# Grouping the row sums with the similarities at the head of an attention pair, and moving the weight sums of the first expert turn

## The chip, the cores and the metric

The kernel runs on one core of a Trainium2 chip. The metric is the device time of one execution in microseconds (us); lower is better. Engines are named as the profile names them: PE is TensorE's matmuls, PEld its weight loads, DVE is VectorE, ACT is ScalarE, POOL is GpSimd, SP is SyncE, which issues most DMAs. [...]

## The reference

Two blocks follow each other. The first is attention with clusters, over 4 batches, 8 heads, 768 positions and 64 features. Each query and each key is assigned to the nearest of 16 centroids, and a query sees only keys of its own cluster. The second is a mixture of experts: each of the 3,072 rows goes to one of 8 experts, which are two matmuls with a ReLU between, and the result is scaled with the gate's weight.

```python
q_assign = np.argmax(np.einsum('bhsd,hcd->bhsc', q_n, c_n), axis=-1)
k_assign = np.argmax(np.einsum('bhsd,hcd->bhsc', k_n, c_n), axis=-1)
mask = q_assign[:, :, :, None] == k_assign[:, :, None, :]
scores = scale * np.matmul(q, k.transpose(0, 1, 3, 2))
scores = np.where(mask, scores, -1000000000.0)
...
attn = attn / (np.sum(attn, axis=-1, keepdims=True) + 1e-09)
return np.matmul(attn, v).astype(np.float32)
...
logits = x @ w_gate
expert_idx = np.argmax(logits, axis=1)
...
for e in range(E):
    h = np.maximum(x_sorted[lo:hi] @ w1[e], 0.0)
    y_sorted[lo:hi] = h @ w2[e]
```

Here x is the attention's output, with the 8 heads of a row side by side (512 features).

## The kernel before

**Pairs.** Attention works on 16 pairs of heads: 4 batches times 4 pairs (`NPAIR`, `HP` = 4). Pair n holds two heads on the two halves of the partitions. Its queries are taken in two halves h (384 columns), its keys in six blocks j (128 each), so a pair has 12 units (h, j), numbered u = 0 to 11. One unit of `score` is four f32 matmuls of queries and keys and two bf16 matmuls that add the mask (all L433), and then an exp on ACT (L445) into a tile A. `add_up` (L451, DVE) adds A into ACC, for the sums over the keys; it runs for all j but 0. After the 12 units come 12 of `attend` (L457), six for each half, each half ended by a copy of the result O from PSUM to the tile oT on ACT (L464).

**What is done beside the pair.** A table, `AT`, holds further steps under (pair, place), and the loop over pairs runs them through `between(n, u)` after unit u; place 12 lies between the two halves of the attends, 13 behind them. The steps are:

- `prepare(n, step)`, for the pair that comes next. Step 0 turns the loaded q and k on DVE (L277, `turn`); step 1 is the matmuls with the centroids (L291, `similar`); step 2 transposes their result out of PSUM and compares it with its maximum (`assign0`, `assign1`, L302 to L311, DVE); step 3 makes the cluster codes ohT (`assign2`, L318 to L327, DVE); steps 4 and 5 copy the codes into the mask tiles mk (L340) and mq (L337), four ACT instructions each. The score's mask matmuls read mk and mq. Step 0 of pair n + 2 is issued in the loop itself, at place 12 of pair n.
- the end of an earlier pair. `sum_up` (L480, 24 PE instructions) forms the softmax sums from ACC and the gate's logits from oT; `weights_of` (L489 to L504, DVE) reads them; `rows` (L510, DVE) turns oT, and `store` (L517, SP) writes it to HBM.
- the gate of a finished batch b: `gate`, `gate_exp` (ACT), `gate_sum`, `choose` (DVE), then `count` (L592, L593, two small matmuls) and `number` (L598 to L607), which gives each row its place in the list of its expert and scatters the row's number to HBM from POOL.
- the preparation of the first expert turn (below).

**PSUM.** The pool `ps_s` has three double banks for scores, so the scores are at most three units ahead of the exps. The pool `ps_m` has two banks for similarities, sums and O. A new tile takes the bank that is released first in the program's order, and waits for that bank's readers. `count` writes into the bank of the latest sums (`BANK`).

**Expert turns.** After attention, 10 turns work through the experts. Turns 0 and 1 take up to 288 rows each of the two fullest experts, from the first three batches. A turn needs: the experts' ranking (`rank_first`, DVE), the list of its rows and the two weights (`first_turns`: `expert`, `places`, `fetch1`, `fetch2`, all on SP), the row indices (`indices`, L728, L729), the gather (`gather`, L738, POOL), the rows times their softmax and gate weights (`weigh`, L755), a way through HBM that splits them (`take`, L771), `turn_rows` (L780, DVE) and the sums and differences that save a matmul in eight (`x_sums` and `w1_sums`, L789, DVE; w1_sums makes A[0] to A[3], where A[1] needs A[2] and A[3] needs A[1]). All of this is placed in pairs 13 to 15 for turn 0.

`layer1` of a turn is 2 x 7 products (L968), with a hook after each, to which steps are tied by number. In turn 0 these hold the sums of pair 15, the gate of batch 3, its count and its numbering. In the first half the products use, in this order: w1 itself, A[2], A[1], w1, A[0], w1, A[3]. The last one adds into a bank that DVE reads first (L926 at L1007).

The loop of the pairs:

```python
for n in range(NPAIR):
    if n + 2 < NPAIR:
        load(n + 2)
    for h in range(2):
        for j in range(NQ):
            score(n, h, j)
            if j:
                add_up(n, h, j)
            between(n, h * NQ + j)
    for h in range(2):
        for j in range(NQ):
            attend(n, h, j)
        if h == 0:
            between(n, 12)
            prepare(n + 2, 0)
    between(n, 13)
```

Of the kernel before, what the change touches and what calls it, by code (L numbers as in the profile page):

```python
# [33 lines left out]
def kernel(  # L34
# [11 lines left out]
    nc = tc.nc  # L46
    B, H, S, D = q.shape
# [8 lines left out]
    HP = H // 2  # L56
    NPAIR = B * HP
# [28 lines left out]
    wa = ctx.enter_context(tc.tile_pool(name="weights_a", bufs=1))  # L86
    w1s = ctx.enter_context(tc.tile_pool(name="w1_sums", bufs=1))
    xp = ctx.enter_context(tc.tile_pool(name="rows", bufs=1))
    accp = ctx.enter_context(tc.tile_pool(name="accp", bufs=3))
    otp = ctx.enter_context(tc.tile_pool(name="otp", bufs=2))  # L90
    stat = ctx.enter_context(tc.tile_pool(name="stat", bufs=2))
    rt = ctx.enter_context(tc.tile_pool(name="route", bufs=1))
# [75 lines left out]
    with tc.manual_schedule(), ExitStack() as actx:  # L168
# [655 lines left out]
        def at_pair(n, u, f, *a):  # L824
            AT.setdefault((n, u), []).append(lambda: f(*a))

        for n in range(NPAIR):
            if n:
                at_pair(n, 2, sum_up, n - 1)
                at_pair(n, 4, rows, n - 1)  # L830
                at_pair(n, 4, store, n - 1)
            for u, step in ((2 if n else 6, 1), (5 if n else 7, 2), (7 if n else 8, 3), (11, 4), (11, 5)):
                at_pair(n, u, prepare, n + 1, step)
        for b in range(B - 1):
            n = HP * (b + 1)
            last = b == B - 2
            at_pair(n, 5 if last else 10, gate, b)
            at_pair(n, 8 if last else 11, gate_exp, b)
            at_pair(n + (not last), 9 if last else 3, gate_sum, b)
            at_pair(n + (not last), 10 if last else 9, choose, b)  # L840
            at_pair(n + 2 - last, 2, count, b)
            at_pair(n + 2 - last, 3 if last else 6, number, b)
        for n in range(1, NPAIR):
            at_pair(n, 2, weights_of, n - 1)
        n = HP * (B - 1)
        slots = range(len(EARLY))
        at_pair(n + 1, 4, rank_first)

        def first_turns():
            for s in slots:  # L850
# [3 lines left out]
            GR[0]["w1"] = fetch1(GR[0]["e"], wa)  # L854
            GR[0]["w2"] = fetch2(GR[0]["e"], wa)

        at_pair(n + 1, 6, first_turns)
        for s in slots:
            at_pair(n + 1, 13, indices, s)
        at_pair(n + 2, 6, gather, 0)  # L860
        at_pair(n + 2, 13, weigh, 0)
        at_pair(n + 3, 1, take, 0)
        at_pair(n + 3, 4, turn_rows, 0)
        at_pair(n + 3, 6, x_sums, 0)
        at_pair(n + 3, 9, w1_sums, 0, (2, 1), nc.vector)
        at_pair(n + 3, 13, w1_sums, 0, (0, 3), nc.vector)

        def between(n, u):
            for f in AT.pop((n, u), ()):
                f()  # L870
# [4 lines left out]
        for n in range(NPAIR):  # L875
            if n + 2 < NPAIR:
                load(n + 2)
            for h in range(2):
                for j in range(NQ):
                    score(n, h, j)  # L880
# [5 lines that stand above are left out]
                    attend(n, h, j)  # L886
                if h == 0:
                    between(n, 12)
                    prepare(n + 2, 0)
            between(n, 13)  # L890
        assert not AT

# [1 line left out]
    with tc.manual_schedule(), ExitStack() as ectx:  # L894
# [262 lines left out]
        n = NPAIR  # L1157
        last = NS - 1
# [6 lines left out]
        def second_weights(s):  # L1165
            GR[s]["w2"] = fetch2(GR[s]["e"], (wa, wb)[s % 2])

        for s in range(NS):
            h1, h2 = {}, {}

            def at(d, i, f, *a):
                d.setdefault(i, []).append(lambda: f(*a))

            if s == 0:
                at(h1, 2, sum_up, n - 1)
                at(h1, 2, weights_of, n - 1)
                at(h1, 3, gate, B - 1)
                at(h1, 3, gate_exp, B - 1)
                at(h1, 5, gate_sum, B - 1)
                at(h1, 5, choose, B - 1)  # L1180
                at(h1, 8, count, B - 1)
                at(h1, 9, number, B - 1)
                at(h1, 11, rows, n - 1)
                at(h1, 11, store, n - 1)
                at(h1, 12, rank_all)
                at(h2, 0, rank_rest)
                at(h2, 3, places, 2)
                at(h2, 3, first_weights, 2)
                at(h2, 5, places, 3)
                at(h2, 7, indices, 2)  # L1190
                at(h2, 7, gather, 2)
            if s == 3:
                at(h1, 12, ask)
                at(h2, 4, answer)
            if s < last:
                if s == 0:
                    first_weights(1)
                elif s > 1:
                    take(s + 1)
                if s == 1:  # L1200
                    at(h1, 6, weigh, 2)
                    at(h1, 7, take, 2)
                    at(h1, 8, second_weights, 2)
                else:
                    second_weights(s + 1)
                if 0 < s <= last - 2:
                    at(h2, 0, first_weights, s + 2)

                if 0 < s <= last - 3:
                    at(h2, 1, places, s + 3)  # L1210

                if s == 0:
                    when = ((h2, 1), (h2, 2), (h2, 5), (h2, 6), (h2, 7), (h2, 7))
                elif s == 1:
                    when = ((h1, 9), (h1, 12), (h2, 2), (h2, 3), (h2, 6), (h2, 6))
                else:
                    when = ((h1, 9), (h1, 10), (h2, 1), (h2, 2), (h2, 2), (h2, 5))
                if GR[s + 1]["T"] >= 2 * P:
                    for (h, i), f, a in zip(when, (w1_sums,) * 4 + (w2_sums,) * 2, (2, 1, 0, 3, 2, 0)):
                        at(h, i, f, s + 1, (a,), nc.vector)  # L1220
                at(h2, 1 if s == 1 else 3, turn_rows, s + 1)
                if GR[s + 1]["T"] >= 2 * P:
                    at(h2, 1 if s == 1 else 4, x_sums, s + 1)
            if s == 0:
                at(h1, 2, gather, 1)
                at(h1, 8, weigh, 1, slice(0, 1))
                at(h1, 11, weigh, 1, slice(1, 2))
                at(h1, 12, weigh, 1, slice(2, 3))
                at(h1, 12, take, 1)
            elif s + 2 <= last:  # L1230
                at(h1, 5 if s == 2 else 4, indices, s + 2)
                at(h1, 5 if s == 2 else 4, gather, s + 2)
                at(h2, 6 if s == 1 else 4, weigh, s + 2)
            if pairs_of(s):
                at(h1, 4, w2_sums, s, (1,), nc.vector)

                at(h1, 5 if s == 1 else 6, w2_sums, s, (3,), nc.vector)
            if s == last - 1:

                at(h1, 4, nc.gpsimd.drain)  # L1240
            (layer1 if GR[s]["T"] >= 2 * P else few_columns)(s, h1)
            h_sums(s)
            layer2(s, h2)
# [271 lines left out]
```

## Time and profile before

| what | us |
|---|---|
| time, median of 3 runs | 660.87 |
| the runs, lowest and highest | 659.3, 662.08 |
| the profiled execution, its own time | 659.27 |
| the profiled execution, its span | 657.5 |
| PE busy | 644.2 (98% of the span) |
| DVE busy | 490.0 (75%) |
| ACT busy | 338.8 (52%) |
| POOL busy | 130.8 (20%) |
| start of pair 1; of turn 0's first layer | 31.8; 329.5 |

The span is the time from the first to the last instruction of the profiled execution; the execution's own time also holds what lies around it. A busy engine isn't one at its peak: the ends of matmuls are modelled, so lengths of PE work are best taken from one start to the next start. TensorE's granted clock was full throughout (0.998). Attention is the first half of the span, the expert turns are the second half.

### The profile page before, as it was taken

Reading aid. Unit: us, or ns where it says so; the run is one execution under the profiler, and the core shown is the slowest. Engines: PE = TensorE matmul, PEld = TensorE weight load, DVE = VectorE, ACT = ScalarE, POOL = GpSimd, SP = SyncE. Lnnn points to the kernel's source line nnn. Section 1 sums busy time; section 2 is a strip of 40 time slices with the busy share of each in tenths; the row PEclk is TensorE's granted clock in tenths of the full one; section 3 lists DMA queues with packets and bytes.
Section 4 is the critical chain, followed back from the end, with each engine's and each line's share of the span. In section 5 each row is a group of like instructions: output and inputs, shape, how many; then the busy total and the mean of one; then the engine's idle time right before and its main releaser. Section 6 shows DMA issues by size and latency. Waiting matters only on the chain.

```text
span 657.5 us, 11491 instructions
## 1 busy us (share of the span) xinstructions
PE 644.2 (98%) x4252; PEld 423.3 (64%) x4252; DVE 490.0 (75%) x845; ACT 338.8 (52%) x584; POOL 130.8 (20%) x166
## 2 busy tenths in 40 slices
PE   8999999999999999999999999999999999999996
PEld 4444544455444454544484979989797987869773
DVE  6988888998889988989887997888869365572300
ACT  4677878768878777867532333333231331323210
POOL 4500000022000300041103522324240422140010
PEclk9999999999999999999999999999999999999999
DMA  7663455443355433347475587776684835614010
GB/s 150 150 120 68 76 94 97 72 80 68 73 97 98 74 76 72 72 132 227 117 273 156 187 314 264 252 275 211 249 307 170 273 138 165 233 74 173 7 49 19
DMA packets 189760, 95.38 MB, mean 145 GB/s; under 512 B 152895, under 2 KB 171839, under 8 KB 188416
## 3 DMA queue, kind: packets, MB, share of 16 engines
q1 hardware_dynamic: 184624, 81.56, 45.2%
q0 software_dynamic: 4928, 12.97, 6.1%
q8 instruction: 35, 0.57, 0.4%
q14 instruction: 29, 0.24, 0.1%
q10 hardware_dynamic: 144, 0.03, 0.0%
HBM read 74.10 MB, written 20.70 MB: 144 GB/s over the span
## 4 chain that ended last, share of the span: by engine, by line
PE 80%; issue 10%; DVE 5%; POOL 2%; ACT 1%; DMA 1%; POOLq 0%; DVEq 0%; ACTq 0%
PE sps L433 20%; PE mps L457 16%; PE bank L968 10%; PE sbank L968 8%; PE bank L1069 7%; PE bank L1088 7%; PE sbank L1069 6%; PE mps L480 2%; PE mps L291 1%; PE bank L937 1%; DMA xg<-x_rows,gi 1%; DVE xT L780 1%; POOL tokens_of L607 1%; DVE acc L451 1%; DVE a L789 1%
## 5 line engine op out<-in xcount | busy, mean ns | idle before, releaser
L445 ACT ACTIVATE A<-sps 128x768 f32<-128x768 f32 x192 | 152.1, 814 | 30.0 <-PE sps L433 29.4
L433 PE MATMUL sps<-qT,kT 64*128 64x384 f32 x768 | 158.9, 492 | 0.0
L451 DVE TENSOR_TENSOR acc<-acc,A 128x768 f32<-128x768 f32 x128 | 121.4, 948 | 11.4 <-ACT A L445 2.9
L457 PE MATMUL mps<-A,v_in 128*64 128x384 f32 x768 | 127.4, 488 | 0.0
L433 PEld LDWEIGHTS sps<-qT,kT 64*128 64x128 f32 x768 | 66.8, 187 | 52.2 <-issue 48.4
L457 PEld LDWEIGHTS mps<-A,v_in 128*64 128x64 f32 x768 | 53.7, 137 | 70.6 <-issue 62.9
L1043 POOL DMA_INDIRECT out_dram<-z,si x30 | 47.7, 1590 | 196.0 <-DVE z L926 167.2
L607 POOL DMA_INDIRECT tokens_of<-tg,pos_i x24 | 27.5, 1147 | 270.5 <-DVE pos_i L605 264.4
L433 PE MATMUL sps<-mq,mk 64*128 64x384 bf16 x384 | 64.9, 323 | 3.1 <-ACT mq L337 1.3
L1088 PE MATMUL bank<-w,h 128*128 128x512 f32 (+2 forms) x224 | 64.4, 596 | 0.0
L340 ACT ACTIVATE mk<-ohT,kscn,ksc 32x384 bf16<-32x384 bf16 x60 | 42.0, 700 | 40.5 <-DVE ohT L327 39.7
L968 PE MATMUL bank<-xT,w 128*128 128x144 f32 (+4 forms) x288 | 47.7, 309 | 0.0
L738 POOL DMA_INDIRECT xg<-x_rows,gi x30 | 38.4, 1280 | 47.0 <-DVE si L729 16.4
L968 PE MATMUL sbank<-xc,a 128*128 128x144 f32 (+4 forms) x288 | 47.7, 309 | 0.0
L1088 PEld LDWEIGHTS bank<-w,h 128*128 128x128 f32 (+2 forms) x224 | 24.6, 151 | 32.5 <-issue 32.3
L968 PEld LDWEIGHTS bank<-xT,w 128*128 128x128 f32 x288 | 43.8, 190 | 2.6 <-issue 2.2
L451 DVE TENSOR_TENSOR acc<-A 128x768 f32<-128x768 f32 x32 | 30.4, 952 | 19.2 <-ACT A L445 19.1
L968 PEld LDWEIGHTS sbank<-xc,a 128*128 128x128 f32 x288 | 43.4, 190 | 0.0
L926 DVE TENSOR_TENSOR h<-sbank,p 128x288 f32<-128x288 f32 (+4 forms) x18 | 9.2, 514 | 45.7 <-PE sbank L968 45.5
L433 PEld LDWEIGHTS <-mk 64*128 64x128 bf16 x384 | 19.9, 94 | 29.0 <-DVE mk L383 2.6
L986 ACT ACTIVATE h<-h 128x288 f32<-128x288 f32 (+4 forms) x36 | 17.6, 488 | 38.1 <-DVE h L926 38.1
L755 DVE TENSOR_TENSOR xw<-xg,sf 128x256 f32<-128x256 f32 (+2 forms) x60 | 32.8, 606 | 0.9 <-DMA xg<-x_rows,gi 0.6
(216 smaller groups left out, 900.5 us busy)
## 6 DMA issues: line engine op xcount, KB each, us to landing
w<-in_moe_w_dram SPq DMA_DIRECT2D x20, 2048.0 KB, 10.7
v_in<-in_v_dram SPq DMA_DIRECT2D x32, 192.0 KB, 2.5
x_rows<-x SPq DMA_DIRECT2D x64, 96.0 KB, 2.4
turn_rows<-xw SPq DMA_DIRECT2D x23, 256.0 KB, 2.0
q_in<-in_q_dram SPq DMA_DIRECT2D x60, 96.0 KB, 3.2
k_in<-in_k_dram SPq DMA_DIRECT2D x60, 96.0 KB, 3.2
xs<-turn_rows SPq DMA_DIRECT2D x16, 144.0 KB, 2.8
xs<-turn_rows SPq DMA_DIRECT2D x8, 208.0 KB, 4.2
```

The costliest lines, as they stand in the source:

```text
L340: nc.scalar.activation(dst, src, AF.Identity, bias=less, scale=big)
L433: nc.tensor.matmul(SP[n, h, j][:, a, 0:HS], lhsT=kt[rows, j * P : (j + 1) * P], rhs=qt[rows, h * HS : (h + 1) * HS], start=first, stop=not ...
L445: nc.scalar.activation(A[n, h, j], ps[:, :, 0:HS], AF.Exp, scale=D**-0.5)
L451: nc.vector.tensor_tensor(ACC[n, h], first, A[n, h, j], op=ALU.add)
L457: nc.tensor.matmul(O[n, h][D * a : D * (a + 1), 0:HS], lhsT=VIN[n][:, a, j, :], rhs=A[n, h, j][:, a, :], start=(j == 0), stop=(j == NQ - 1),)
L607: ins = nc.gpsimd.indirect_dma_start(out=t_d[:, :], out_offset=bass.IndirectOffsetOnAxis(ap=pos_i[:, i : i + 1], axis=0), in_=tg[:, b, i, ...
L738: nc.gpsimd.indirect_dma_start(out=xg[0:m], out_offset=None, in_=x_d[0:rows_in, :], in_offset=bass.IndirectOffsetOnAxis(ap=g["gi"][0:m, j ...
L755: nc.vector.tensor_tensor(xw[0:m, :, :, d2 * a : d2 * (a + 1)], xg[0:m].rearrange("p (r a d b) -> p a r b d", r=HP, a=2, b=DB)[:, a], g["s ...
L968: nc.tensor.matmul(ps[:, f * T2 : (f + 1) * T2], lhsT=w[:, k, (2 * j + f) * P : (2 * j + f + 1) * P], rhs=x[:, k, :], start=first and f + ...
L1043: ins = nc.gpsimd.indirect_dma_start(out=out[:, :], out_offset=bass.IndirectOffsetOnAxis(ap=GR[s]["si"][0:rows, j : j + 1], axis=0), in_=z ...
L1069: nc.tensor.matmul(ps[:, 0:H], lhsT=x[:, k, :], rhs=y[:, k, :], start=first and k == 0, stop=k == 3, skip_group_check=not first,)
L1088: nc.tensor.matmul(ps[i * m : (i + 1) * m, :], lhsT=h[:, f, j * P : j * P + m], rhs=w[:, f, :], start=(k == 0), stop=(k == FB // n - 1),)
```

## The change

Seven things change, all of them places of work; no instruction's work itself is changed.

1. There is a new place, -1, ahead of a pair's first score (`between(n, -1)`).
2. In pairs 2 to 11 `sum_up` of the pair two back and `similar` of the next pair are issued at place -1. `weights_of` follows at 0, `rows` and `store` at 3. The steps assign0/1, assign2 and the turn of pair n + 2 are at 2, 4 and 9 (before: 5, 7, 12). For this, ACC has four buffers instead of three. In pair 1 nothing is summed.
3. Pair 12 sums pair 10 at -1 (its rows at 0), and then pair 11 at 2, with the similarities. From pair 13 on a pair sums the one before it at 2, as before the change; `weights_of` comes at 3 there.
4. The gates of batches 0 and 1 come about one pair later, with `count` at place 2 of pairs 7 and 11.
5. `rank_first` and `first_turns` in pair 13 move from 4 and 6 to 9 and 11, `indices` from the end of pair 13 to place 2 of pair 14; `weigh` and `take` are issued at 11 and 13 of pair 14.
6. In pair 15 the weight sums A[2], A[1], A[0], A[3] are at 1, 2, 3, 4 (before: two at 9, two at 13), `turn_rows` and `x_sums` at 6 and 7 (before: 4 and 6).
7. In turn 0 the sums of pair 15 and their weights move from hook 2 to hook 3, the gate of batch 3 from hook 3 to hook 4.

```diff
-    accp = ctx.enter_context(tc.tile_pool(name="accp", bufs=3))
+    accp = ctx.enter_context(tc.tile_pool(name="accp", bufs=4))
...
+        LATE = HP * (B - 1)
+
+        def pair_end(n, u, v, m):
+            at_pair(n, u, sum_up, m)
+            at_pair(n, u + 1, weights_of, m)
+            at_pair(n, v, rows, m)
+            at_pair(n, v, store, m)
+
         for n in range(NPAIR):
-            if n:
-                at_pair(n, 2, sum_up, n - 1)
-                at_pair(n, 4, rows, n - 1)
-                at_pair(n, 4, store, n - 1)
-            for u, step in ((2 if n else 6, 1), (5 if n else 7, 2), (7 if n else 8, 3), (11, 4), (11, 5)):
-                at_pair(n, u, prepare, n + 1, step)
+            if n >= 2 and n <= LATE:
+                pair_end(n, -1, 3 if n < LATE else 0, n - 2)
+            if n >= LATE:
+                pair_end(n, 2, 5 if n == LATE else 4, n - 1)
+            if n == 0:
+                steps = (6, 7, 8, 11, 11, 12)
+            elif n == 1 or n >= LATE:
+                steps = (2, 5, 7, 11, 11, 12)
+            else:
+                steps = (-1, 2, 4, 11, 11, 9)
+            for step, u in enumerate(steps):
+                at_pair(n, u, prepare, n + 1 + (step == 5), (step + 1) % 6)
         for b in range(B - 1):
             n = HP * (b + 1)
             last = b == B - 2
-            at_pair(n, 5 if last else 10, gate, b)
-            at_pair(n, 8 if last else 11, gate_exp, b)
-            at_pair(n + (not last), 9 if last else 3, gate_sum, b)
-            at_pair(n + (not last), 10 if last else 9, choose, b)
-            at_pair(n + 2 - last, 2, count, b)
-            at_pair(n + 2 - last, 3 if last else 6, number, b)
-        for n in range(1, NPAIR):
-            at_pair(n, 2, weights_of, n - 1)
+            if last:
+                when = ((n, 5), (n, 8), (n, 9), (n, 10), (n + 1, 2), (n + 1, 3))
+            else:
+                when = ((n + 1, 10), (n + 1, 13), (n + 2, 3), (n + 2, 9), (n + 3, 2), (n + 3, 6))
+            for (m, u), f in zip(when, (gate, gate_exp, gate_sum, choose, count, number)):
+                at_pair(m, u, f, b)
         n = HP * (B - 1)
         slots = range(len(EARLY))
-        at_pair(n + 1, 4, rank_first)
+        at_pair(n + 1, 9, rank_first)
...
-        at_pair(n + 1, 6, first_turns)
+        at_pair(n + 1, 11, first_turns)
         for s in slots:
-            at_pair(n + 1, 13, indices, s)
+            at_pair(n + 2, 2, indices, s)
         at_pair(n + 2, 6, gather, 0)
-        at_pair(n + 2, 13, weigh, 0)
-        at_pair(n + 3, 1, take, 0)
-        at_pair(n + 3, 4, turn_rows, 0)
-        at_pair(n + 3, 6, x_sums, 0)
-        at_pair(n + 3, 9, w1_sums, 0, (2, 1), nc.vector)
-        at_pair(n + 3, 13, w1_sums, 0, (0, 3), nc.vector)
+        at_pair(n + 2, 11, weigh, 0)
+        at_pair(n + 2, 13, take, 0)
+
+        for u, i in enumerate((2, 1, 0, 3)):
+            at_pair(n + 3, u + 1, w1_sums, 0, (i,), nc.vector)
+        at_pair(n + 3, 6, turn_rows, 0)
+        at_pair(n + 3, 7, x_sums, 0)
...
                 load(n + 2)
+            between(n, -1)
             for h in range(2):
...
                     between(n, 12)
-                    prepare(n + 2, 0)
             between(n, 13)
...
             if s == 0:
-                at(h1, 2, sum_up, n - 1)
-                at(h1, 2, weights_of, n - 1)
-                at(h1, 3, gate, B - 1)
-                at(h1, 3, gate_exp, B - 1)
+                at(h1, 3, sum_up, n - 1)
+                at(h1, 3, weights_of, n - 1)
+                at(h1, 4, gate, B - 1)
+                at(h1, 4, gate_exp, B - 1)
```

## The prediction

> **What bounds the kernel now.** I read the page's busy shares first: PE 98%, DVE 75%, ACT 52%. So the end is set by TensorE's stream, and only two things can move it: work that PE does, and places where PE stands. The chain of waits, narrowed to one ordinary pair, shows the stream (start, length, in us):
>
> ```profile
> 170.20 2.62 PE sps L433 x18
> 172.82 1.11 PE mps L480 x24
> 173.93 0.65 PE mps L291 x8
> 174.58 7.47 PE sps L433 x54
> 182.05 7.89 PE mps L457 x48
> 189.94 0.84 PE sps L433 x3
> ```
>
> One pair is 3 score units, sums (L480), similarities (L291), 9 score units, 12 attends: 19.74 us, nothing else on the chain. Next, busy time in five stretches: pair 8, pair 13, pair 14, pair 15, and the first layer of turn 0.
>
> ```profile
> core 0: us, PE busy (x) PEld busy (x) DVE busy (x) ACT busy (x) POOL busy (x), PEclk, DMA share, GB/s
> 170.13:189.87 19.74, 19.74 (x155) 9.66 (x153) 17.05 (x29) 15.59 (x23) 0.00 (x0) 1.00 0.46 83
> 268.96:288.84 19.88, 19.88 (x156) 9.77 (x154) 18.21 (x45) 11.90 (x18) 6.77 (x6) 1.00 0.21 45
> 288.84:310.37 21.53, 20.21 (x154) 9.89 (x152) 19.49 (x37) 17.47 (x27) 4.58 (x4) 1.00 0.76 254
> 310.37:329.47 19.10, 19.10 (x146) 9.41 (x145) 15.88 (x27) 11.70 (x17) 2.26 (x2) 1.00 0.40 100
> 329.47:347.20 17.73, 16.76 (x144) 15.13 (x143) 14.69 (x37) 6.08 (x16) 2.04 (x3) 1.00 0.68 253
> ```
>
> Only pair 14 (21.53) and turn 0 lose time; every other pair is full, and DVE is at 17 to 19 of 19.7, so it has little room. The timelines of ACT, DVE and PE say why (idle time before the row in brackets):
>
> ```profile
> 287.43 2.85 ACT L340 ACTIVATE mk<-ohT,kscn,ksc 32x384 bf16<-32x384 bf16 x4 [5.56 <-DVE ohT L327]
> ```
> ```profile
> 290.86 0.32 PE L433 MATMUL sps<-mq,mk 64*128 64x384 bf16 x1 [1.10 <-ACT mq L337]
> ```
> ```profile
> 338.75 1.25 PE L968 MATMUL sbank<-xT,a 128*128 128x144 f32 x8 [0.71 <-DVE h L926]
> ...
> 342.16 0.17 PE L592 MATMUL mps<-last,lt_b 128*128 128x8 bf16 x1 [0.21 <-DVE last L586]
> ```
>
> In pair 13 DVE gives the cluster codes (ohT) late, ACT copies them into the mask late, and pair 14's first mask matmul stands. Its three scores take 4.42 (288.84 to 293.26) for the usual 2.62: 1.8 us lost. In turn 0, PE waits behind DVE's queue.
>
> [...]score units start 0.807 us apart (155.68, 156.49, 157.29), so nine are 7.26, but the stretch of nine takes 7.47 and that of three 2.62 instead of 2.42. Each separate run of scores costs 0.20 to 0.21. [...]ACT stood 5.56 us before a mask copy with other work behind it. [...]
>
> **Part 1, the head group, pairs 2 to 11.** Sums (of pair n-2) and similarities stand before the first score, so attend, sums, similarities and twelve scores follow. Scores: 12 x 0.807 + 0.21 = 9.89 instead of 2.62 + 7.47 = 10.09. The 128-row group keeps its 1.76, attends their 7.89 (the same 7.89 stands before L902, another mode, so its exit doesn't depend on the follower). Pair: 19.54. Gain 0.20 x 10 = 2.0 us. Bounds from the bubble: 0.1 to 0.3 each.
>
> Does the head stand on something? Sums take the bank of O(h=0), freed by ACT's copy after the eight mask copies (5.0 us). With the assigns at 2 and 4, DVE reaches the codes after four adds instead of six: first add at 4.6 after the head, once two exps exist (weights_of, 1.35, lies before it), then four adds of 0.87, or 1.05 where the next one depends on it, assigns 1.67 and 2.07, rows 0.89: 12.9. Copies run 13.0 to 18.0, O(0) is out at 18.4, the next head is at 19.5: no wait. Similarities need O(1)'s copy, 0.65 after the head (329.58 + 0.48 against 329.47), and come at 1.0: no wait. Their turn, at u = 9, comes after four more adds and ends at 18.5. No cover is left if codes slip by 1.1 us.
>
> **Part 2, count of batches 0 and 1** moves to pairs 7 and 11 at u = 2, now alone inside scores. Today it costs 0.14 beside the similarities (134.89 to 135.03) in pairs 6 and 10. Alone it also splits scores: 0.14 + 0.20. Net +0.40 (between +0.2 and +0.8).
>
> **Part 3, sums moved over pairs.** Pair 1 loses its sums: 1.76 becomes 0.78 (pair 0's similarities alone), -0.98. Pair 12 gets an extra head of sums alone, 1.11 as in pair 15. Net +0.13.
>
> **Part 4, pairs 12 to 14.** Pair 12 does two pairs' ends. weights_of(10) and rows(10), 2.24 us of DVE, fit into its idle 1.68 before the first add plus its wait for the fourth exp. But weights_of(11) now follows add 3 instead of filling that wait. From add 3 DVE never idles: today 255.62 to 272.11, the second turn's end, is 16.49. With weights_of 1.35 more, 17.84, starting at 1.11 + 2.62 + 1.76 + 2.01 = 7.50 after the head, it ends at 25.34; pair 13 starts at 1.11 + 19.74 = 20.85. Hence: mask copies start 3.01 before pair 13 (codes at 7.50 + 10.23, plus 0.11). Today a start 1.41 before pair 14 costs 1.79, so the break is 3.20: stall 0.19. Sums follow 2.81 into the pair, similarities at 3.81, but the turn ends at 4.49: stall 0.74. Together +0.93.
>
> Pair 13: score 4 starts 5.46 in, add 3 at 7.47. Then add 0.87, weights_of 1.08, number 1.35, add 0.88, rows 0.90, add 0.87, assign 1.74, add 0.87, assign2 2.06: codes at 18.09 (rank_first, 2.18, now behind them). The pair lasts 19.74 + 0.14 + 0.93 = 20.81; copies start 2.66 before its end: stall 0.54. Adds 1.90, rank 2.18, adds 1.90: sums wait until 3.32 into pair 14 (0.16), similarities until turn(15)'s end at 5.06 + 0.06 (0.80). Together 1.50, against 1.79 today: -0.29.
>
> Moved DMAs. first_turns follows the ranking (at 22.2 of pair 13). Its register loads, four list loads and two weight loads took 287.49 to 291.35 until the second list landed; with about 1.5 for register reads no longer hidden by the token wait, that is 6.9 into pair 14. SP's x_rows store of pair 13 comes at 12, so nothing stands behind. Indices reach DVE at 6.9: no margin, but DVE then waits for exp 4 at 7.9, which hides 0.3. Gather landed 9.75 after its index (293.49 to 303.24), so 17.5, weigh at 21.5. w1 took 7.4: 12.5 into pair 14, wanted 4.5 into pair 15. Take and weigh keep their place on DVE; SP's take still precedes store(14).
>
> **Part 5, pair 15 and turn 0.** Four weight sums of 1.22 go between adds, turn_rows waits no more for its DMA (2.48 of DVE today). DVE ends its last add 23.5 after the pair's start; sums at hook 3 start at 23.7. Today: 333.16 to 334.82 = 1.66 for 1.11, so 0.55 goes. Then c (338.75): before it 0.88 is lost; weights_of now lies beside the product and gate behind the add, 0.1 remains. But DVE's weights_of-to-choose chain took 6.25 (335.86 to 342.11), still about 6.0, and PE now reaches the count 5.0 after it: about 1.05 for 0.21 today. Net -0.55 - 0.78 + 0.84 = -0.5 (from -1.3 to 0). Experts after that keep their order: nothing.
>
> **Sum.** -2.0 + 0.40 + 0.13 + 0.93 - 0.29 - 0.5 = -1.3 us. The profiled execution took 659.27 (span 657.5 plus 1.8 around it), so 657.9; it is the low end of the runs, whose median is 660.87, so the median goes to 659.5.
>
> **Rivals.** (B) The late pairs come out clean: the 0.93 of pair 13, the 1.50 of pair 14 and 0.2 of the count wait don't appear, because the spread of rank and sums lets DVE get by. For it: each is a wait of under 1 us, so a DVE order 1 us quicker removes nearly all. Against: 17.8 us of DVE work without a gap. -1.3 - 2.6 = -3.9: 657.0.
> (C) Slower: DVE stands before indices in pair 14 for a late list. Price: lists on a loaded queue take 10.0 us to land by the page instead of 1.8 to 2. That is 8 later; DVE absorbs 1, and codes for pair 15 have 0.65 to spare (copies start 3.85 before it, break 3.20), so PE loses about 6.4: 660.87 - 1.3 + 6.4 = 666.0. It ends slower than before once the lists are 3 us late, by over 0.5% once 6.3. Against it: the loads are issued ahead of the weights.
> (D) The change doesn't do what it says: [...]part 1 is nothing: +0.7, 661.6. Against it: 7.89 before L902.
>
> **Numbers.** Forecast 0.42, B 0.38, C 0.10, D 0.10. B gets this much since DVE tallies of three loaded pairs multiply small errors, and all of them are waits that a little shift removes. Half a percent is 3.3 us, about what a measurement of this kernel tells from no change. Forecast and D fall within: 0.52; B faster: 0.38; C slower: 0.10. The forecast's own range is 658.0 to 661.0. The range 655.8 to 662.0 takes in B, D and both ends of parts 1, 2 and 5, and leaves C out.
>
> **What would show it.** Part 1: pairs 2 to 11 at 19.54, one score stretch of 9.9, no PE gap before L480. Part 2: 19.9 in pairs 7 and 11. Part 4: waits of L291 for the turn (L277) at pairs 13 and 14, and mask waits under 1. Part 5: L480 in turn 0 at 1.1, a longer wait at L592. Wrong, if a head pair stays at 19.7, if PE waits for ACT's copy (L464) in the heads, or if the lists land late.

## The result, and the profile after

The changed kernel took 662.29 us (median of 13 runs, 661.33 to 663.20) beside 660.87 of the kernel before (13 runs, 658.64 to 662.08): ratio 1.0028, 95% interval 1.0018 to 1.0038, or by the medians 1.4 us longer where 1.3 less was forecast. That is one comparison. A second one of the same two kernels gave 658.48 for 659.45: ratio 0.9987 (interval 0.9980 to 0.9995; ratios below are to the kernel before in the same comparison and are written in this way). A third gave 663.06 for 660.47: 1.0034 (1.0025 to 1.0043). The second and the third ran on two different chips; on which the first ran is not known. Most of what follows is about why they differ.

The page of the profiled execution of the first comparison (span 660.6, own time 662.30), its busy shares and its chain that ended last:

```profile
PE 645.3 (98%) x4252; PEld 424.2 (64%) x4252; DVE 488.7 (74%) x845; ACT 340.2 (51%) x584; POOL 131.9 (20%) x166
PE 76%; DVE 15%; ACT 4%; issue 2%; DMA 1%; SPq 1%; DVEq 0%; POOL 0%; POOLq 0%; ACTq 0%
```

TensorE is as busy as before. DVE's share of the chain is 15%; in the second comparison's profile of the same kernel it is 9%. Where the time goes is seen in busy time of the stretches that the prediction showed (pairs 8, 13, 14, 15, first layer of turn 0; the columns are those of the table shown there):

```profile
168.50:189.63 21.13, 19.82 (x155) 9.68 (x153) 17.12 (x26) 14.99 (x22) 3.08 (x4) 1.00 0.42 76
269.44:290.74 21.30, 21.09 (x156) 10.05 (x155) 18.94 (x41) 15.02 (x23) 7.15 (x6) 1.00 0.33 62
290.74:312.11 21.37, 21.16 (x155) 10.11 (x153) 18.31 (x43) 14.39 (x22) 4.48 (x4) 1.00 0.66 236
312.11:332.44 20.33, 19.57 (x147) 9.62 (x145) 19.89 (x30) 13.36 (x21) 2.26 (x2) 1.00 0.51 116
332.44:349.06 16.62, 16.02 (x143) 14.99 (x142) 12.01 (x36) 5.99 (x16) 2.04 (x3) 1.00 0.71 270
```

The same stretches of the same kernel in the second comparison (span 656.4):

```profile
168.12:187.66 19.54, 19.54 (x155) 9.72 (x153) 17.12 (x27) 15.39 (x22) 3.07 (x4) 1.00 0.46 83
267.46:288.30 20.84, 20.84 (x157) 9.97 (x155) 18.47 (x40) 14.59 (x22) 7.14 (x6) 1.00 0.30 58
288.30:309.67 21.37, 21.16 (x155) 10.12 (x153) 18.86 (x44) 15.02 (x23) 3.94 (x4) 1.00 0.65 235
309.67:329.45 19.78, 19.57 (x146) 9.61 (x145) 19.39 (x30) 13.05 (x20) 2.31 (x2) 1.00 0.53 121
329.45:346.08 16.63, 16.03 (x144) 15.00 (x143) 12.03 (x36) 6.00 (x16) 2.05 (x3) 1.00 0.71 270
```

Turn 0 and pair 14 agree to 0.01 us. Pair 8 differs by 1.59, pair 13 by 0.46, pair 15 by 0.55. With 0.35 in pair 2 and 1.15 in turn 3 (both below) this is all of the 4.1 us between the two spans. The chain of waits around pair 8's head (start, length, what), first comparison:

```profile
168.57 1.11 PE mps L480 x24
169.69 0.65 PE mps L291 x8
170.33 3.07 PE sps L433 x18
173.40 0.01 issue
173.41 0.82 ACT A L445
174.22 0.04 issue
174.27 7.54 PE sps L433 x54
```

and second comparison:

```profile
168.19 1.11 PE mps L480 x24
169.30 0.65 PE mps L291 x8
169.95 9.89 PE sps L433 x72
```

In the second the head is what Part 1 predicted: one stretch of twelve score units, 9.89. In the first, the fourth score unit waits for the first exp (L445), which began at 173.41 although the last matmul of its scores had started at 171.02; in the second it began 0.4 us behind that matmul. TensorE was on time, ScalarE heard of it 2 us late. VectorE did too: the transposed sums (L489) came 2.46 us after the last matmul of the sums, 0.71 in the second.

One more thing sets the two profiles apart, in the landing times of DMAs. First comparison and second:

```profile
w<-in_moe_w_dram SPq DMA_DIRECT2D x20, 2048.0 KB
```
```profile
w<-in_moe_w_dram SPq DMA_DIRECT2D x20, 2048.0 KB, 11.9
```

The first has no landing times, because records of semaphore updates are missing in it. (Such a record in the profile gives the time at which an engine or a DMA reported that something is ready.) 7,984 updates are recorded, for 8,909 in the second and 8,966 in the kernel before's profile. Most of the missing ones are DMAs' (5,909 for 6,770), but PE, ACT and DVE lack 13, 14 and 32 too. Of these three engines' 1,722 updating instructions 49 have no record within 0.4 us of their end. All 49 lie within 0.5 us of an indirect transfer of POOL (token scatters L607, gathers, row writes), where only 405 of the 1,722 lie. All nine profiles here from three chips (those of the third comparison, of scatter_over_9 and of turns_9) lost hundreds of records in this way; in each of the eight from two others at most two engine updates lack theirs.

The records that are there also show where the 2 us come from: TensorE's updates themselves are late. At this head its last sums, its similarities and its first three score units ended at 169.69, 170.33, 171.34, 172.15 and 172.95; its updates are recorded at 171.80, 173.25, 173.32, 173.40 and 173.47, and the exp began 0.09 us after the third of these, its own. In the second profile every one is recorded within 0.04 us of the end. VectorE's and ScalarE's recorded updates at the first profile's head are on time (within 0.03 us). The same holds throughout: up to 650 us, updates recorded more than 0.15 us behind the end of the last instruction that can have made them are TensorE's alone, 3 to 20 of them in each of the ten profiles with losses, and none in the nine without.

### The profile page after: what moved, and what is told of

The parts are those of the page before. It is cut to its first block, busy times and chain, and to the rows that moved or that the text cites. A ratio compares the mean times of both kernels' runs of the same rounds, so it can differ in the third digit from the quotient of the medians.

```text
span 660.6 us, 11502 instructions
## 1 busy us (share of the span) xinstructions
PE 645.3 (98%) x4252; PEld 424.2 (64%) x4252; DVE 488.7 (74%) x845; ACT 340.2 (51%) x584; POOL 131.9 (20%) x166
## 4 chain that ended last, share of the span: by engine, by line
PE 76%; DVE 15%; ACT 4%; issue 2%; DMA 1%; SPq 1%; DVEq 0%; POOL 0%; POOLq 0%; ACTq 0%
PE sps L433 17%; PE mps L457 13%; PE bank L983 11%; PE sbank L983 9%; PE bank L1103 7%; PE bank L1084 7%; PE sbank L1084 6%; DVE acc L451 4%; PE mps L480 2%; ACT mk L340 2%; DVE xT L780 1%; PE mps L291 1%; PE bank L952 1%; DVE a L789 1%; ACT mq L337 1%
## 5 line engine op out<-in xcount | busy, mean ns | idle before, releaser
L445 ACT ACTIVATE A<-sps 128x768 f32<-128x768 f32 x192 | 151.8, 812 | 37.8 <-PE sps L433 37.2
L457 PE MATMUL mps<-A,v_in 128*64 128x384 f32 x768 | 127.4, 488 | 0.0
L457 PEld LDWEIGHTS mps<-A,v_in 128*64 128x64 f32 x768 | 53.7, 137 | 70.6 <-issue 63.7
L607 POOL DMA_INDIRECT tokens_of<-tg,pos_i x24 | 27.5, 1144 | 272.4 <-DVE pos_i L605 266.3
L738 POOL DMA_INDIRECT xg<-x_rows,gi x30 | 39.6, 1319 | 47.3 <-DVE si L729 25.2
```

The source lines that it names most:

```text
L445: nc.scalar.activation(A[n, h, j], ps[:, :, 0:HS], AF.Exp, scale=D**-0.5)
L457: nc.tensor.matmul(O[n, h][D * a : D * (a + 1), 0:HS], lhsT=VIN[n][:, a, j, :], rhs=A[n, h, j][:, a, :], start=(j == 0), stop=(j == NQ - 1),)
L607: ins = nc.gpsimd.indirect_dma_start(out=t_d[:, :], out_offset=bass.IndirectOffsetOnAxis(ap=pos_i[:, i : i + 1], axis=0), in_=tg[:, b, i, ...
L738: nc.gpsimd.indirect_dma_start(out=xg[0:m], out_offset=None, in_=x_d[0:rows_in, :], in_offset=bass.IndirectOffsetOnAxis(ap=g["gi"][0:m, j ...
```

## The experiments

**Two repeats and two edits on a chip whose profiles lose no records.** The changed kernel and the kernel before, unedited:

> The changed kernel once more, nothing edited: what of its profile is the kernel's own and what belongs to one execution. If the late signals at the heads of pairs 8 and 12 belong to the kernel, pair 8 takes about 21.5 us from start to start again (its first sixteen score units 11.5, exp 1 starting some 2.4 us after the second matmul of unit 1 instead of 0.4) and pair 12 shows the same lag. If they were an accident of that execution (rival), both heads have the 0.4 us lag of the other pairs, pair 8 takes about 19.9, and the span is about 1.6 shorter. Pair 15's late mask (about 1.2 us) and the two stalls at the start of pair 13 (0.7 and 0.8) repeat in both theories.

> The kernel before once more, nothing edited: how far two profiles of one kernel stand apart, and whether the expert turns after the first (from the second layer of turn 0 to the end) take the same time twice. Theory that the 1.2 us by which the changed kernel's expert turns were longer belongs to the execution: this profile's expert turns differ from the first profile's by something like 1 us, most of it between 410 and 440 us. Theory that it belongs to the change: they agree within 0.3 us. The attention stage agrees within 0.2 us in both.

657.97 and 659.28 us in one profiled execution each, beside a single 660.4 of the kernel before. Pair 8 took 19.54 from first weighted value (L457) to first weighted value. So the late head belongs to the circumstances of the execution and not to the program alone. The kernel before repeated its attention to 0.1 us and its expert turns to 0.3.

Numbering moved:

```diff
-                when = ((n + 1, 10), (n + 1, 13), (n + 2, 3), (n + 2, 9), (n + 3, 2), (n + 3, 6))
+                when = ((n + 1, 10), (n + 1, 13), (n + 2, 3), (n + 2, 9), (n + 3, 2), (n + 4, 6) if b == 0 else (n + 3, 3))
```

> The changed kernel with the numbering of batch 0, and so POOL's six token scatters, one pair later (pair 8, unit 6, so that they run over the head of pair 9), and that of batch 1 three units earlier (pair 11, unit 3, so that they end before the head of pair 12). Theory 'POOL's scatters over a head hold up what the other engines hear of TensorE': the heads of pairs 8 and 12 have the usual lag of 0.4 us and pair 8 takes about 19.9 us, and the head of pair 9 gets the lag of some 2.3 us and takes about 21.1 instead of 19.54. Theory 'the count in the pair before does it, whatever POOL is at': pairs 8 and 12 stay as they are, pair 9 stays at 19.54. Theory 'an accident of the execution': none of the three is late.

663.49 us, and it decides nothing on its question: no record was missing, and the edit did something else. (The two numberings moved, the counts stayed.) The count's PSUM bank, one of two, is read by the numbering, so it was held over a pair, and pair 7's weighted values stood for the copy of O out of the other one (below, scatter_over_9 moves both, and nothing stands there):

```profile
PE mps L457 <- ACT oT L464: 2.4, 1, 2.4
```

Indices later in pair 14:

```diff
-            at_pair(n + 2, 2, indices, s)
+            at_pair(n + 2, 5, indices, s)
```

> The changed kernel with the early turns' indices taken three score units later in pair 14 (unit 5 instead of 2, still ahead of the gather at 6). Theory 'VectorE standing in the indices for the lists of tokens is what delays the mask copies of pair 15': the two waits of 0.85 and 1.28 us at the indices shrink to at most 0.3 in sum, the mask copies for pair 15 start about 3 us before the pair instead of 1.97, and the three scores at the start of pair 15 take 2.7 to 3.0 us instead of 3.92; the span is 0.9 to 1.2 us shorter. Rival 'ScalarE's own exps set the mask copies': the waits shrink but the copies start where they did, and the 1.2 us stays.

657.7 us, and pair 15's three scores took 2.62 us, as in the kernel before. Timed beside the changed kernel, on the chip of the second comparison:

> The changed kernel unedited, timed in five rounds. The single run of it above took 657.97 us beside 660.4 of the kernel before, where thirteen runs had given 662.29 beside 660.87. Theory 'the changed kernel's schedule gains 1 to 2 us, and an execution can lose 2 to 4 us in the attention pairs on top of it': the median is near 658 to 659 us, 0.2 to 0.4 per cent under the kernel before, if this chip doesn't disturb it, and the undisturbed profile shows pair 8 at 19.54 us. Rival 'the single run was a lucky one': the median is again about 662 us, and most executions lose the 2 us at pair 8.

> The changed kernel with the early turns' indices at unit 5 of pair 14 instead of 2, timed. In its single profile the three scores at the start of pair 15 took what they take in the kernel before. Theory 'the wait at the indices is worth what the profile shows': 0.5 to 1.2 us less than the changed kernel beside it. Rival: within 0.3 us of it, because the disturbances are larger than the gain.

The changed kernel took 658.48 us, 0.9987 (0.9980 to 0.9995); with the indices later 658.11, 0.9979 (0.9971 to 0.9988). The difference in the profiles, 0.69 us in pair 15, is one wait of VectorE for a list, here in the changed kernel's second profile:

```profile
DVE gi L728 <- DMA sf<-tokens_of: 1.5, 1, 1.5
```

The medians show 0.4 of it, with intervals that overlap.

**The parts alone**, on the same chip. turn0_only is the kernel before with the new places of weigh, take, w1_sums, turn_rows and x_sums and the last pair's steps at hooks 3 and 4; group_only is the changed kernel with these put back.

> The kernel before with the second part of the change alone: the weight sums of turn 0 at units 1 to 4 of the last pair, its rows and input sums after them at 6 and 7, the weighing and the take of pair 14 earlier, and the last pair's own steps one hook later in the first turn. Theory 'this part is worth the 1.1 us by which the first layer of turn 0 is shorter, and costs nothing in the attention': the first layer of turn 0 takes 16.6 us instead of 17.7, and the time is 0.9 to 1.3 us under the kernel before. Rival 'weighing at unit 11 and the sums in the last pair delay what TensorE waits for': pairs 14 and 15 get longer by as much, and the time doesn't move.

> The changed kernel with the turn-0 part put back as it was before (weight sums at units 9 and 13 of the last pair, weighing, take, rows and input sums in their old places, the last pair's steps at the old hooks). Theory 'the head group gains 2.0 us in ten pairs and gives back about as much in pairs 2, 7, 11, 13, 14 and 15': within 0.8 us of the kernel before. Rival 'the head group is what the time is lost by': 1 to 3 us over the kernel before, with the loss at the heads of pairs 8 and 12.

turn0_only: 658.43, 0.9989 (0.9977 to 1.0001, which takes in no change at all), first layer of turn 0 at 16.6 us. group_only: 660.51, 1.0016 (1.0006 to 1.0026). The head group by itself is a loss of about 1 us even where no signal is late. Its attention, from the first weighted value of pair 0 to that of pair 15, took 297.92 us for 297.66 before: what the heads gain is given back there. 0.39 is lost in the first layer of turn 0, whose first three products take 0.58 longer (the count itself is as before), 0.33 in that of turn 1. The rival was right in sign, but not about pairs 8 and 12. The two parts do not add up to the whole: by the medians -1.0 and +1.1, where both together gave -1.0. Those 0.39 and 0.33 are part of it, for the whole's profile has neither; the rest is not explained.

**A third comparison, and rows behind the codes.** rows_late has the indices at 5 and:

```diff
-                pair_end(n, -1, 3 if n < LATE else 0, n - 2)
+                pair_end(n, -1, 3 if n < LATE else 9, n - 2)
-                pair_end(n, 2, 5 if n == LATE else 4, n - 1)
+                pair_end(n, 2, 13 if n < NPAIR - 1 else 4, n - 1)
```

turn0_rows is turn0_only with rows and store of pairs 11 to 13 at place 13 instead of 4.

> The changed kernel unedited, timed once more beside the kernel before, on whatever chip this falls. Its comparison on record gave a ratio of 1.0028 (a profile of 660.6 us with some 900 semaphore records missing in it, at the very places where signals of TensorE came 2 us late), and the one above 0.9987 (a profile with none missing). Theory 'the loss at pairs 8, 12 and 15 and in the third turn came from outside the kernel': ratio 0.997 to 1.000 again, pair 8 at 19.54 us. Rival 'the changed kernel loses it whenever chance has it so, and half of all comparisons come out slower': a ratio over 1.001 in this one.

> The changed kernel with the indices at unit 5 of pair 14 and, besides, the transposes of the pair's rows in pairs 12, 13 and 14 put behind the codes and the next pair's turn (pair 10's from place 0 of pair 12 to 9, those of pairs 11, 12 and 13 from 5 and 4 to the pair's end). Theory 'pairs 13 and 14 stand because VectorE's codes and turns come 0.2 to 0.8 us late behind these transposes of 0.97 us each': the mask stalls (0.2 and 0.67) and the similarities' waits (0.75 and 0.77) go or fall under 0.2 each, pair 13 takes about 19.9 us instead of 20.83 and pair 14 about 19.9 instead of 21.37; the time is 1.5 to 2.4 us under the indices alone (658.11). Rival 'ScalarE's own queue sets the copies' or 'the wait moves on to the next pair': under 0.5 us gained.

> The kernel before with the turn-0 part of the change (658.43 us, 0.9989, alone) and the same rows of pairs 11, 12 and 13 put to the pair's end; no head group. Theory: pair 14's stall of 1.71 us at its masks, which the kernel before has too, falls to under 0.7, and the time is 1.0 to 1.7 us under turn0_only. Rival: the codes of pair 14 are late for the numbering and the ranking of pair 13, not for the rows, and less than 0.5 us is gained.

after_third: 663.06, 1.0034 (1.0025 to 1.0043), pair 8 at 21.29 us, 7,910 records. The rival's number came true, by the first theory's cause: this chip loses records. rows_late: 661.58, 1.0010 (1.0001 to 1.0019), 1.5 us under the changed kernel beside it. Pair 14 fell from 21.60 to 20.63; its wait at the mask, 0.68 of that, is gone. Pair 13 stayed at 21.2, but not with the same waits: its three scores fell from 3.19 to 2.62, so its mask wait went too, and its sums rose from 1.00 to 1.55, because the additions that they read now came behind a transpose of the rows (L510). The wait moved on.

turn0_rows: 659.81, 0.9986 (0.9975 to 0.9998), with pair 14 at 22.68 for 21.53 in the kernel before. That is not because the rows did nothing: the three scores took 3.32 for 4.41, so the mask wait fell from 1.79 to 0.70, about as far as the theory had it. But gathers (L738) ran from 292.9 to 298.3, over the scores behind, and there TensorE waited for an exp:

```profile
PE sps L433 <- ACT A L445: 1.1, 1, 1.1
PE sps L433 <- issue: 0.4, 1, 0.4
PE sps L433 <- ACT mq L337: 0.2, 1, 0.2
```

The update of the score unit that ended at 296.24 is recorded at 298.89, and its exp began at 298.97. The nine score units took 9.71 for 7.47. So a late signal took back what the rows had gained, behind gathers this time and not behind token scatters.

**Is it POOL's scatters over the head?** scatter_over_9 moves batch 0's count and numbering by one pair, both, so that no bank is held; batch 1 is the control. scatters_early takes both numberings to unit 3:

```diff
+                m = n + 4 if b == 0 else n + 3
-                when = ((n + 1, 10), (n + 1, 13), (n + 2, 3), (n + 2, 9), (n + 3, 2), (n + 3, 6))
+                when = ((n + 1, 10), (n + 1, 13), (n + 2, 3), (n + 2, 9), (m, 2), (m, 6))
```
```diff
-                when = ((n + 1, 10), (n + 1, 13), (n + 2, 3), (n + 2, 9), (n + 3, 2), (n + 3, 6))
+                when = ((n + 1, 10), (n + 1, 13), (n + 2, 3), (n + 2, 9), (n + 3, 2), (n + 3, 3))
```

> The changed kernel with the count and the numbering of batch 0 one pair later (pair 8, units 2 and 6, for pair 7), so that POOL's six token scatters of that batch run over the head of pair 9; batch 1 stays, with its scatters over the head of pair 12. Theory 'on some chips the signals between the engines come 2 us late while POOL's indirect transfers run, and the change has put the scatters over two heads': where the profile of this run has semaphore records missing, pair 8 takes 19.54 us, pair 9 gets the loss of 1.6 to 1.9 us (21.1 to 21.4, with the count's own 0.34 moved from pair 7 to pair 8), and VectorE's logits of the head of pair 12 still come 2 us late. Where none is missing, pair 9 takes 19.54. Rival 'pair 8 itself is late, whatever POOL is at': 21.1 to 21.4 in pair 8, 19.54 in pair 9.

> The changed kernel with the numbering of batches 0 and 1 at unit 3 of pairs 7 and 11 instead of 6, so that the scatters start and end about 4 us earlier against the heads of pairs 8 and 12. Theory: on a chip with late signals the head of pair 8 falls back to under 20.2 us (from 21.2) and the mask stall of pair 13 to 0.2; 1.2 to 2.5 us less than the changed kernel, ratio 0.997 to 1.002. On a chip without: as the changed kernel, 0.998 to 0.9995. Rival 'the lag follows the scatter to wherever it ends, and costs the same over the weighted values of pair 7': no change.

This chip, another one, loses records as well. scatter_over_9: 661.96, 1.0031 (1.0014 to 1.0047). Its chain at the head of pair 9:

```profile
187.52 1.11 PE mps L480 x24
188.63 0.65 PE mps L291 x8
189.28 3.17 PE sps L433 x18
192.45 0.01 issue
192.45 0.82 ACT A L445
193.27 0.04 issue
193.32 7.54 PE sps L433 x54
```

The loss has gone with the scatters: pair 9 takes 21.23, pair 8 takes 19.88 with the count's 0.34 in it, and the transposed sums of pair 12's head, the control, come 2.61 us after their matmuls. With both scatters early, the head of pair 8 in the same comparison:

```profile
168.77 1.11 PE mps L480 x24
169.88 0.65 PE mps L291 x8
170.53 9.89 PE sps L433 x72
```

659.73 us, 0.9989 (0.9980 to 0.9998), though the profile still loses records (7,952): 2.2 us under scatter_over_9. So on this kind of chip the loss at a head goes with the numbering and its transfers, not with pair 8, and not with the count, which stayed in pair 7 here. The numbering's own work on VectorE moved along, so the edits don't part it from POOL's transfers; but it stands at the same place in the second comparison's profile, where no head is late.

**A version that is faster than both on chips that lose records**, and the turn-0 part again. rows_scatters is rows_late with the numberings at 3.

> The changed kernel with three edits: the numbering of batches 0 and 1 at unit 3 of pairs 7 and 11, the indices at unit 5 of pair 14, and the rows of pairs 10 to 13 behind the codes. If their gains add up it is faster than both kernels on either kind of chip: ratio 0.995 to 0.9975 on one without late signals, 0.997 to 0.9995 on one with them. Rival: the late signals take the gain again in pairs 13 and 14, whose own scatters and gathers stay where they are, and it is level with the kernel before.

> The kernel before with the turn-0 part alone, as above (0.9989 on a chip without missing records), beside the others of this call. Theory: it leaves the scatters where the kernel before has them, so its gain of 0.7 to 1.3 us is the same on either kind of chip, ratio 0.998 to 0.999. Rival: the gathers and the scatter of the first turn, which it leaves beside the weight sums, take it back on a chip with late signals: ratio 0.9995 to 1.001.

rows_scatters: 658.15, 0.9972 (0.9963 to 0.9981), where the changed kernel had 1.0028 and 1.0034 in other comparisons; on a chip without losses it was not run. turn0_again: 659.66, 0.9989 (0.9980 to 0.9999), the same as on the other kind of chip. What TensorE still waits for in rows_scatters is in pair 14's chain (and likewise in pair 13), 0.77 us at the similarities:

```profile
288.39 2.62 PE sps L433 x18
291.01 1.25 PE mps L480 x24
292.26 1.42 PE mps L291 x8
```

turns_9 puts the turn (L277) of pairs 12 and 13 at unit 9 instead of 12, ahead of the gate sums and the choice (and pair 10's rows at 10).

> The version with the three edits (numbering of batches 0 and 1 at unit 3, indices at unit 5, rows behind the codes; 658.15 us, 0.9972) with a fourth: in pairs 12 and 13 the turn of the pair after next at unit 9 instead of 12, ahead of batch 2's sum of gates and choice, with pair 10's rows one unit later. In the profile of that version TensorE still waits 0.75 us for the turned keys in pairs 13 and 14, because VectorE has 3 us of rows, gate sums and choice ahead of the turn. Theory: both waits go, the similarities take 0.83 us again, pairs 13 and 14 take about 20.1 and 19.9 us instead of 20.83 and 20.65, and the time falls by 1.2 to 1.6 us beside the same version. Rival 'VectorE is then late with what comes behind the turn' (the additions of the last units, and the weight sums' turn at the start of the next pair): the gain is under 0.5 us.

> The version with the three edits once more, for the comparison with turns_9 on one chip, and on another chip than before if it so falls: ratio 0.9965 to 0.998 if the gain belongs to the kernel; 0.998 to 1.000 if the chip of the last call favoured it.

turns_9 lost 4.5 us: 662.78, 1.0034 (1.0022 to 1.0047), beside 658.28, 0.9969 (0.9959 to 0.9979), of rows_scatters on the same chip. TensorE's waits of turns_9 say why (1.1 of these 3.1 in pair 13, 1.4 in pair 14, 0.5 in turn 0; besides, pair 14's three scores take 3.62 for 2.62, for a late mask):

```profile
PE mps L480 <- DVE acc L451: 3.1, 3, 1.4
```

The keys are there, but the additions behind them are now late for the sums, which stand ahead of the similarities. Like rows_late's pair 13, this shows VectorE short of time over these pairs: the order picks what is late, and of these two orders the old one picked the cheaper.

## Why the prediction was wrong, and where it was right

**The step that failed is Part 2.** It cost the count of batches 0 and 1, moved to pairs 7 and 11, at +0.40, which is what TensorE pays (19.88 for pairs 7 and 11). The numbering that moves with it, and the six token scatters that POOL issues behind it, it put at nothing without following them. Before, they ran at 143.9 to 152.7 and 223.0 to 231.8, over the starts of pairs 7 and 11, where nothing is lost even with late signals (19.74 in turn0_again); now at 163.8 to 172.5 and 243.9 to 252.4, over the heads of 8 and 12. The first and the last of batch 0's six, before and after:

```profile
143.89 1.67 POOL L607 DMA_INDIRECT tokens_of<-tg,pos_i  x1 [117.79 <-DVE pos_i L605]
...
151.71 0.97 POOL L607 DMA_INDIRECT tokens_of<-tg,pos_i  x1 [0.30 <-DMA tokens_of<-tg,pos_i]
```
```profile
163.81 1.67 POOL L607 DMA_INDIRECT tokens_of<-tg,pos_i  x1 [137.72 <-DVE pos_i L605]
...
171.52 0.97 POOL L607 DMA_INDIRECT tokens_of<-tg,pos_i  x1 [0.30 <-issue]
```

Part 1's "no wait" at the head was worked out with VectorE's and ScalarE's own times; nothing in the trace of before shows that an engine can hear of TensorE 2 us late. Where that happens, pair 8 pays 1.6 to 1.9 us and pair 13 some 0.4, and with the scatters off the heads the time is 2.2 us less (661.96 to 659.73). Pair 15's 0.55 does not belong here: on the chip of the third comparison, with losses, it took 19.54.

**The link to the median** failed with it. The profile of before has all its records, like those of the chips without losses, and its 659.27 is near the 659.45 of the second comparison; on the three chips with losses the kernel before took 660.34 to 660.52. The prediction took it for the low end of one distribution. By these medians late signals may cost the kernel before about 1 us too; this is not shown, for there is no profile of it with losses. Turn 3's first layer is one place where they cost (turns count from 0): it took 13.72 us in the profiles without losses, 14.19 in turn0_again, and 14.87 in the changed kernel's first profile, with late updates of TensorE and this wait in it:

```profile
PE sbank L983 <- ACT sbank L1016: 0.9, 1, 0.9
```

**The sum itself** held where no signal was late: -1.3 forecast, -0.9 measured (0.9987; -0.3 to -1.3 by the interval), -1.1 between profiles. In part that is luck: two terms were off by some 0.6 each, pair 15 upwards and Part 5 downwards, and cancel. Its terms, from the second comparison's profile:

| term | predicted | measured |
| --- | --- | --- |
| Part 1, a head pair | 19.54 | 19.54 in eight pairs, 19.88 with a count |
| Part 2 on TensorE | +0.40 | +0.40 |
| Part 3, pair 1 / pair 12 | -0.98 / +1.11 | -0.97 / +1.11 |
| Part 4, pair 13: mask, similarities | 0.19 + 0.74 | 0.21 + 0.75 |
| Part 4, pair 14: mask, sums, similarities | 0.54 + 0.16 + 0.80 | 0.68 + 0.18 + 0.78 |
| pair 15 | 0 | +0.69 |
| Part 5, first layer of turn 0 | -0.5 | -1.1 |

Pair 15 is rival C's mechanism at a tenth of its price: VectorE stood 1.5 us for a list, "no margin" was right, and the cover of 0.65 us that the codes had was used up; indices_5 removed it. Part 5's error is mostly its last term: the wait at the count came to 0.60, not 1.05, so +0.39 for +0.84. Its middle term gave 0.94 for 0.78; the sums' 0.55 came true. "No wait" for ScalarE's copies failed once: in some profiles, the first among them, the sums of pair 2's head wait 0.29 us for L464, and the pair takes 19.90.

**The rivals.** B (late pairs clean) fell: pairs 13 and 14 of the changed kernel kept their waits in every profile. Another order took away one of them, pair 14's 0.68 at the mask (rows_late, rows_scatters); in pair 13 it moved the wait, and turns_9's order lost. C came true in kind, not in size. D fell: the 0.20 that a separate run of scores had cost is saved, pair after pair (19.54 for 19.74). None of the rivals was late signals; the one that ended slower had its place in pair 14, and the largest loss was in pair 8.

**Open.** What differs between the chips is not known, nor why records are lost where signals are late. At the first profile's head the late updates are recorded close together (173.25, 173.32, 173.40 and 173.47, so 0.07 to 0.08 us apart). No run here was without a recorder, so whether recording has a part in it is not shown.

## What to carry to other kernels

When a step moves, follow its consequences to the last engine: the count cost TensorE 0.4 us as predicted, but the scatters that POOL issues behind the numbering, four units later, landed on the head of a pair, where TensorE soon waits for an exp that waits for TensorE. Keep indirect transfers off such places, even where one profile shows them free: pair 8's head cost nothing in the second comparison, 1.6 to 1.9 us on the chips with losses. When an edit gains nothing, look at its own wait before dropping it: turn0_rows did cut 1.1 us at the mask, and lost it elsewhere. And before a profile is taken as the baseline of a sum, see whether its own time lies in the middle of the comparison's runs: here it lay 1.6 us aside, more than the whole forecast.

## What the runs showed of the hardware

A short stall can be paid twice. In number_moved TensorE stood 2.4 us, and its clock was then granted at half for 3.41 us (columns as above; the granted clock is the number ahead of the DMA share):

```profile
164.00:166.00 2.00, 0.65 (x4) 0.00 (x0) 1.90 (x3) 1.95 (x5) 0.00 (x0) 1.00 0.92 145
166.00:168.00 2.00, 0.98 (x6) 0.48 (x8) 1.93 (x3) 0.94 (x2) 0.00 (x0) 1.00 0.80 122
168.00:170.00 2.00, 2.00 (x10) 0.78 (x8) 0.96 (x1) 0.00 (x0) 0.00 (x0) 0.53 0.38 61
170.00:172.00 2.00, 2.00 (x12) 0.77 (x10) 0.00 (x0) 0.00 (x0) 0.00 (x0) 0.62 0.00 0
```

The second half of pair 7's weighted values took 5.8 us for 3.9: 12.25 in all for 7.96, of which 2.4 is the stall and 1.9 the clock. A stall of 1.6 us (rows_late, at 172.9) did not bring it, nor one of 1.3 us in the first comparison's profile (at the same time; 1.00 granted around it). The length of one stall is not all, though: in six profiles, this one among them (mean granted clock 0.993 to 0.996, in the others 0.997 to 0.999), the half rate also stands for 3.41 us at some 14 to 18 us, with no stall of over 1.5 us ahead of it.
